# A linear-attention layer beside a long convolution on one core: dense scratch rows, D inside the filter, and a new table of priorities

## The chip, the cores and the metric

The kernel runs on one core of a Trainium2 chip. The time is device microseconds (us) of one execution; three executions of the kernel before are given, and one further execution was recorded by the hardware profiler. The engines are TensorE (PE; PEld is its loading of weights), VectorE (DVE), ScalarE (ACT), GpSimd (POOL) and SyncE (SP, which here issues all DMAs; SPq is its queue).

## The reference

Two independent parts, whose outputs stand side by side in the last axis (576 columns each, 2048 positions, bf16).

```python
# part A, 32 heads of 18, four segments of L = 512 positions
for s in range(4):
    logits = qs @ ks.T * scale + mask            # causal within the segment
    a_dot = softmax(logits) @ vs
    a_mem = (phi(qs) @ M) / (phi(qs) @ z + 1e-6) # phi(t) = t+1 if t>0 else exp(t)
    o = g * a_mem + (1 - g) * a_dot              # g = sigmoid(beta), one per head
    M += phi(ks).T @ vs ;  z += phi(ks).sum()
a = concat(o) @ wo
# part B, 576 channels, 2048 positions
kv = causal_conv4(k, shift_k) * v
y  = irfft(rfft(kv, 4096) * rfft(ssm_k, 4096))[:2048] + kv * ssm_D
b  = q * y
```

## The kernel before, in words

A small planner at build time holds both parts as one graph of operations. Each operation has its engines to choose from (a copy out of PSUM may go to VectorE or ScalarE), an estimated duration for each, and a priority: its place in its part's list, scaled to 0..0.9 for part A and 0..1 for part B. The planner picks, of the operations that could start soonest, the one with the lowest priority number, and so writes a fixed order for each engine. Nothing is reordered on the chip: an engine's instructions, and the DMAs on a queue, run in the order written.

Part A, for each segment s: x is loaded transposed (`xT`, L356, by transposing DMAs), q and k are projected (`pq`, L380), copied to SBUF (`q`, L245 on VectorE, L246 on ScalarE; these two lines are the copy helper for all tiles), stored to a DRAM scratch (`a_qk_scratch`, L368; k also to `a_k_scratch`, L372, from where it is read back transposed for the memory, `phiK`, L434) and read back so that each head lies on its own 32 partitions (`qk`, L408). V is projected on its own (`pv`, L417). The 32 heads are worked in four pairs of groups of four heads; the pair p holds the groups 2p and 2p+1. For each pair ten score tiles (`sc`, L483) go through an exponential (`PT`, L486, ScalarE, 160 in all) and masks on GpSimd (L491, 112 in all), then to the products with V (`po`, L530) and with the memory (`pn`, L537), whose sums ride along as a 19th column. `norm` gathers these sums from SBUF (`cs`, L555) and stores the outputs to `a_o_scratch` (L561, four DMAs per pair). `weights` inverts the sums on VectorE (L577), writes the factors to `a_r_scratch`, and a DRAM to DRAM copy (L588) spreads each factor over its head's 18 rows in `a_rx_scratch`. `dense` reads five tiles of 128 rows of outputs (`nt`, L604) and factors (`rt`, L606), multiplies (L612) and adds (L613), and `out_proj` multiplies with wo (`pout`, L624).

Part B splits 576 channels into three groups g of 192. The taps of the short convolution run on TensorE (`pc`, L816) over k that a transposing DMA has loaded (`kv`, L808). The long convolution is a Fourier transform in two stages: the first (`pf`, L839, two blocks of 256 columns per PSUM tile) gives `A_h` for the filter and `A_kv` for the signal. The second is done in 16 rows k1 per group, 48 in all:

```python
ph = self.f2(A_h, k1, 0, 1, Hs)                       # TensorE, L853
nc.vector.tensor_tensor(out=Hs[:, 1:3, :], in0=ph[:], in1=DI[:], op=ALU.add)     # L877: + D
eng.tensor_scalar(out=Hs[:, 0, :], in0=Hs[:, 2, :], scalar1=-1.0, ...)           # L881: -Im
px = self.f2(A, k1, 1, 0, X)                          # then a copy to X, L245 or L246
eng.tensor_tensor(out=Y.., in0=X.., in1=win, op=ALU.mult)       # L893, GpSimd, 4 x 192
eng.tensor_tensor(out=Y[:, 2:4, :], in0=Y[:, 0:2, :], in1=Y[:, 2:4, :], op=ALU.add)  # L898
```

L881 and L898 may go to GpSimd or VectorE; 45 of 48 stand on VectorE. The inverse of a row (`pi`, L865) writes over `A_kv`. When all 16 rows of a group are there, six blocks of transposes (`pt`, L913), a small product (`py`, L918) and the multiplication with q (`q_sb`, L921) end the group.

Buffers are rings: `big` (three) holds the index tables for the sines at the start, the `kv` tiles, `A_h` and `A_kv`, given out in the order in which the tiles are named; PSUM has two double slots for the scores and four single ones for all else.

## Time and profile before

| | |
|---|---|
| three executions | 377.89 us median, 376.07 to 379.33 |
| profiled execution | 379.78 us, of which 378.1 from the first to the last instruction |
| busy | PE 303.4, DVE 300.7, ACT 244.2, POOL 180.5 us |
| granted TensorE clock, mean | 0.905 |
| moved by DMA | 59.79 MB, 108604 packets, all from SyncE's queue |

Busy time is the union of an engine's instructions. A group's line gives the line of the program, the engine, what is written and read, the number, then busy us and mean ns of one, then the engine's idle time ahead of them with what ended it. A line of the timeline gives start and length in us. 1.7 us of the execution lie outside the span.

### The profile page before, as it was taken

Reading aid. Unit: us, or ns where it says so; the run is one execution under the profiler, and the core shown is the slowest. Engines: PE = TensorE matmul, PEld = TensorE weight load, DVE = VectorE, ACT = ScalarE, POOL = GpSimd, SP = SyncE. Lnnn points to the kernel's source line nnn. Section 1 sums busy time; section 2 is a strip of 40 time slices with the busy share of each in tenths; the row PEclk is TensorE's granted clock in tenths of the full one; section 3 lists DMA queues with packets and bytes.
Section 4 is the critical chain, followed back from the end, with each engine's and each line's share of the span. In section 5 each row is a group of like instructions: output and inputs, shape, how many; then the busy total and the mean of one; then the engine's idle time right before and its main releaser. Section 6 shows DMA issues by size and latency. Waiting matters only on the chain.

```text
span 378.1 us, 8137 instructions
## 1 busy us (share of the span) xinstructions
PE 303.4 (80%) x3030; PEld 171.8 (45%) x3052; DVE 300.7 (80%) x559; ACT 244.2 (65%) x337; POOL 180.5 (48%) x206
## 2 busy tenths in 40 slices
PE   0969695799988939799997988678997877789536
PEld 0524453355445514565453544234554443557413
DVE  8615574888999978877789997976889999998940
ACT  3621774688889846779876557685897886583202
POOL 7100120457678654415468535553638887673000
PEclk9978877899999997999998799898998998698957
DMA  6997889957325468639536877981543555224871
GB/s 138 224 213 196 186 170 176 234 154 194 98 71 112 83 183 188 177 104 226 150 103 153 185 214 211 236 252 53 124 129 101 166 146 150 80 81 135 248 217 63
DMA packets 108604, 59.79 MB, mean 158 GB/s; under 512 B 79508, under 2 KB 100692, under 8 KB 108564
## 3 DMA queue, kind: packets, MB, share of 16 engines
q1 hardware_dynamic: 108564, 59.26, 63.7%
q8 instruction: 24, 0.39, 0.4%
q14 instruction: 16, 0.13, 0.1%
HBM read 29.68 MB, written 23.82 MB: 142 GB/s over the span
## 4 chain that ended last, share of the span: by engine, by line
PE 33%; DVE 27%; DMA 16%; SPq 8%; ACT 7%; issue 7%; POOL 0%; DVEq 0%; ACTq 0%
DMA rt<-a_rx_scratch 6%; PE pout L624 5%; PE sc L483 5%; PE po L530 4%; PE pq L380 4%; DMA qk<-a_qk_scratch 4%; PE pp L853 3%; DVE Y L898 3%; ACT PT L486 3%; PE pi L865 3%; DVE nt L612 3%; DVE Hs L877 3%; SPq L808 2%; PE pf L839 2%; PE pv L417 2%
## 5 line engine op out<-in xcount | busy, mean ns | idle before, releaser
L486 ACT ACTIVATE PT<-sc 128x1024 bf16<-128x1024 f32 x160 | 157.7, 1034 | 39.1 <-PE sc L483 26.6
L491 POOL TENSOR_SCALAR_AFFINE_SELECT PT<-PT 128x512 bf16<-128x512 bf16 (+1 forms) x112 | 84.5, 768 | 101.7 <-ACT PT L486 95.9
L893 POOL TENSOR_TENSOR Y<-X,Hs 128x768 bf16<-128x768 bf16 x48 | 80.3, 1674 | 53.6 <-DVE X L245 19.8
L483 PE MATMUL sc<-qk 18*128 18x384 bf16 (+3 forms) x512 | 58.9, 316 | 9.7 <-ACT PT L486 4.8
L380 PE MATMUL pq<-xT,wqk 128*128 128x512 bf16 x161 | 47.0, 406 | 4.3 <-DVE ou L245 2.1
L483 PEld LDWEIGHTS <-qk 18*128 18x128 bf16 x512 | 16.2, 93 | 44.3 <-issue 38.8
L865 PE MATMUL pi<-Y,CST 128*128 128x192 bf16 x96 | 25.4, 265 | 10.5 <-DVE Y L898 8.7
L624 PE MATMUL pout<-wo_sb,od 128*128 128x288 bf16 x160 | 26.6, 319 | 8.6 <-DVE od L613 5.4
L839 PE MATMUL pf<-W1bd,xs 128*128 128x256 bf16 x144 | 27.3, 318 | 7.0 <-DVE V L245 3.1
L246 ACT CAST q<-pq 128x512 bf16<-128x512 f32 x23 | 13.5, 587 | 27.0 <-PE pq L380 20.9
L530 PE MATMUL po<-PT,V 128*32 128x256 bf16 (+3 forms) x512 | 27.1, 336 | 3.0 <-DVE Hs L877 1.8
L898 DVE TENSOR_TENSOR Y<-Y 128x384 bf16<-128x384 bf16 x45 | 28.6, 636 | 0.7 <-POOL Y L893 0.6
L877 DVE TENSOR_TENSOR Hs<-pp,DI 128x384 bf16<-128x384 f32 x48 | 26.3, 548 | 1.9 <-PE pp L853 1.7
L380 PEld LDWEIGHTS <-wqk 128*128 128x128 bf16 x180 | 17.3, 103 | 23.0 <-issue 9.8
L819 DVE TENSOR_TENSOR kv<-pc,kv 128x512 bf16<-128x512 f32 x20 | 13.5, 687 | 17.3 <-PE pc L816 17.3
L816 PE MATMUL pc<-kv,dg 128*128 128x512 bf16 x77 | 21.5, 422 | 5.8 <-ACT q L246 3.7
L853 PE MATMUL pp<-A_h,CS 128*128 128x192 bf16 x96 | 24.3, 256 | 1.8 <-DVE Hs L877 1.1
L853 PE MATMUL pp<-A_kv,CS 128*128 128x192 bf16 x96 | 24.5, 259 | 1.2 <-DVE X L245 0.4
L881 DVE TENSOR_SCALAR Hs<-Hs 128x192 bf16<-128x192 bf16 x45 | 23.5, 521 | 1.3
L246 ACT CAST oA<-pout 128x288 bf16<-128x288 f32 x25 | 10.0, 398 | 22.1 <-PE pout L624 21.2
L624 PEld LDWEIGHTS <-od 128*128 128x128 bf16 x160 | 16.5, 107 | 16.8 <-DVE od L613 6.6
L417 PE MATMUL pv<-wv,xT 128*128 128x288 bf16 x160 | 24.0, 293 | 0.0
(134 smaller groups left out, 575.4 us busy)
## 6 DMA issues: line engine op xcount, KB each, us to landing
qk<-a_qk_scratch SPq DMA_DIRECT2D x48, 108.0 KB
nt<-a_o_scratch SPq DMA_DIRECT2D x15, 256.0 KB
rt<-a_rx_scratch SPq DMA_DIRECT2D x15, 256.0 KB
a_o_scratch<-ou SPq DMA_DIRECT2D x48, 72.0 KB
xs<-in_B_ssm_k_dram SPq DMA_DIRECT2D x3, 768.0 KB
xs<-kv_scratch SPq DMA_DIRECT2D x3, 768.0 KB
q_sb<-in_B_q_dram SPq DMA_DIRECT2D x3, 768.0 KB
out_dram<-oA SPq DMA_DIRECT2D x16, 144.0 KB
```

The costliest lines, as they stand in the source:

```text
L380: nc.tensor.matmul(pq[:], lhsT=self.wqk[:, t, 128 * m:128 * m + P], rhs=xT[:, t, :], start=(t == 0), stop=(t == 4)) for t in range(5)],
L483: nc.tensor.matmul(ps[:, b, off:off + n], lhsT=qk[r, 2 + u, P * kt:P * kt + P], rhs=qk[r, u, P * kt:L], start=True, stop=True, tile_positi ...
L486: self.act(act_us(1024), lambda: nc.scalar.activation(out=dst(), in_=ps[:], func=ACT.Exp, scale=self.scale), r=[ps], w=[key])
L491: self.pool(0.2 + n * 0.13, lambda: nc.gpsimd.affine_select(out=ap(), in_=ap(), compare_op=ALU.is_ge, fill=0.0, base=0, pattern=[[0, n], [ ...
L530: nc.tensor.matmul(po[32 * j:32 * j + 32, P * kt:L], lhsT=V[:, kt, 19 * h:19 * h + 32], rhs=rhs, start=(kt == 0), stop=(kt == 3), tile_pos ...
L624: nc.tensor.matmul(ps[:], lhsT=o[:, t, P * qt:P * qt + P], rhs=self.wo[:, t, 288 * h:288 * h + 288], start=(t == 0), stop=(t == 4)) for t ...
L839: self.G.op([(PEQ, pe_us(256, 256), lambda cc=cc, ps=ps: [nc.tensor.matmul(ps[:, u, :], lhsT=xs[:, cc + u, :], rhs=self.W1[:].rearrange("p ...
L853: nc.tensor.matmul(pp[:, o, :], lhsT=tab[:, k1, :], rhs=A[:, 16 * n + k1, :], start=(n == 0), stop=(n == 1))
L865: nc.tensor.matmul(pp[:, o, :], lhsT=tab[:, k1, :], rhs=Y[:, 2 + n, :], start=(n == 0), stop=(n == 1))
L877: self.dve(dve_us(2 * GB), lambda: nc.vector.tensor_tensor(out=Hs[:, 1:3, :], in0=ph[:], in1=DI[:], op=ALU.add), r=[ph, (DI, 0), (DI, 1)], ...
L893: eng.tensor_tensor(out=Y[:].rearrange("p (x h) c -> p x h c", x=2), in0=X[:].unsqueeze(2).to_broadcast([P, 2, 2, GB]), in1=win, op=ALU.mult)
L898: return lambda: eng.tensor_tensor(out=Y[:, 2:4, :], in0=Y[:, 0:2, :], in1=Y[:, 2:4, :], op=ALU.add)
```

## The change: what it does

- Part B, row: D is added to the first tap of the filter (`xs`, L993, three small additions) ahead of its transform, so L877 and the tile `DI` go. The spectra of filter and signal are copied plain into one tile `HX` (two copies of 384, VectorE or ScalarE). No negative is made; instead of one sum of 384, GpSimd does a difference and a sum of 192 each (L953, L954), on GpSimd alone.
- Part B, first stage: four blocks per tile instead of two (36 copies of 1024 instead of 72 of 512), in the two double PSUM slots that the scores use.
- Part A: pair p holds the groups p and p+4. Scratches hold heads densely; k is read for `phiK` from the same scratch as q, and `a_k_scratch` goes. A pair's outputs, sums included, go to DRAM in one DMA; the sums are gathered from there (for the last pair from SBUF, as before). `dense` takes tiles of 7 heads (126 rows, the last 72) and reads the factors from `a_r_scratch`, each row 18 times; `a_rx_scratch` goes. wo is reordered to match by a copy through DRAM.
- Start: the first segment's x is one plain load, transposed on TensorE (20 transposes). Some loads may be issued from ScalarE's queue. The filter of group 0 is transformed ahead of the convolution taps.
- Planner: several estimated durations are raised or lowered, part A is scaled to 0..0.8, and two tables, keyed by stage, move priorities (`SHIFT`, 196 entries) and the choice of engine for copies (`BIAS`, 60 entries; the number is added to ScalarE's finishing time when the planner compares).

```diff
     def kloop(self, A_h, A, g, k1):
...
-        Hs = Tl(pl.H, [P, 3, GB], BF16, "Hs")
-        ph = self.f2(A_h, k1, 0, 1, Hs)
-        DI = self.DI
-        self.dve(dve_us(2 * GB), lambda: nc.vector.tensor_tensor(
-            out=Hs[:, 1:3, :], in0=ph[:], in1=DI[:], op=ALU.add), r=[ph, (DI, 0), (DI, 1)], w=[(Hs, 1)])
...
-        self.G.op([(POOLQ, 0.35, neg(nc.gpsimd)), (DVEQ, 0.17, neg(nc.vector))], r=[(Hs, 1)], w=[(Hs, 0)])
-
-        X = Tl(pl.X, [P, 2, GB], BF16, "X")
-        px = self.f2(A, k1, 1, 0, X)
-        self.copy(2 * GB, lambda: X[:], lambda: px[:], r=[px], w=[X, (A, "x", k1)])
+        HX = self.f2(A_h, A, k1)
...
-        self.G.op([(POOLQ, 1.75, mul(nc.gpsimd))], r=[X, (Hs, 0), (Hs, 1)], w=[Y])
-        self.G.op([(POOLQ, 0.95, add(nc.gpsimd)), (DVEQ, 0.33, add(nc.vector))], w=[Y])
+        def addsub():
+            nc.gpsimd.tensor_tensor(out=Y[:, 0, :], in0=Y[:, 0, :], in1=Y[:, 3, :], op=ALU.subtract)
+            nc.gpsimd.tensor_tensor(out=Y[:, 1, :], in0=Y[:, 1, :], in1=Y[:, 2, :], op=ALU.add)
+        self.pool(1.7, mul, r=[(HX, 0), (HX, 1)], w=[Y])
+        self.pool(1.1, addsub, w=[Y])
...
+    def f2(self, A_h, A, k1):
...
+            for x, src in enumerate((A_h, A)):
+                pp = self.psj([P, 1, L], "pp")
+                self.pe(pe_us(*[GB] * 4), lambda x=x, src=src, pp=pp: emit(0, src, pp), r=keys(src), w=[pp])
+                self.copy(2 * GB, lambda x=x: HX[:, x, :], lambda pp=pp: pp[:, 0, 0:2 * GB], r=[pp],
+                          w=[(HX, x)] + ([(A, "x", k1)] if x else []))
...
     def f1(self, xs, A):
+        w = 4 if F1D else 2
...
+            ps = Tl(self.pl.pss, [P, 4, 256], F32, "pf") if F1D else self.psj([P, 2, 256], "pf")
...
     def begin(self, g):
+        self.dve(0.15, lambda: nc.vector.tensor_tensor(out=xs[:, :, 0], in0=xs[:, :, 0], in1=self.Dt[:, n * g:n * g + n],
+                                                       op=ALU.add), r=["Dt"], w=[xs])
...
     def av(self, s, p, u):
-        hg = 2 * p + u
+        hg = p + 4 * u
...
     def norm(self, s, p):
+        dst = bass.AP(od.tensor, od[256 * p:256 * p + 1].offset, [[W, P], [128 * W, 2], [1, W]])
+        self.dma(256 * nk, lambda dq: dq.dma_start(out=dst, in_=ou[:].rearrange("p u k n -> p u (k n)")),
+                 r=[(ou, u, k) for u in range(2) for k in range(nk)], w=[("od", s, p)])
...
     def dense(self, s, t):
+        rsrc = bass.AP(rd.tensor, rd[7 * t:7 * t + 1].offset, [[W, nh], [0, DH], [1, W]])
...
+    def first_x(self, ident):
+        x = Tl(self.pl.big, [P, 4, D], BF16, "x0")
+        self.dma(576, lambda dq: dq.dma_start(out=x[:], in_=self.A_x[0, 0:L, :].rearrange("(t p) c -> p t c", p=P)), w=[x])
...
-    rank(G.ops[n0:n1], 0.0, 0.9)
-    rank(G.ops[n1:], 0.0, 1.0)
+    rank(G.ops[n0:n1], 0.0, 0.8, SHIFT)
+    rank(G.ops[n1:], 0.0, 1.0, SHIFT)
+    G.bias = BIAS
```

What the orders look like. SyncE's queue at the start, before (from its first row on):

```order
L294 DMA wqk<-in_A_wq_dram 128x4x576
L295 DMA wqk<-in_A_wq_dram 64x576
L356 DMA_TRANSPOSE xT<-in_A_x_dram 128x512 x5
L294 DMA wqk<-in_A_wk_dram 128x4x512
L295 DMA wqk<-in_A_wk_dram 64x512
...
L808 DMA_TRANSPOSE kv<-in_B_v_dram 128x2048
L808 DMA_TRANSPOSE kv<-in_B_k_dram 128x2048
L368 DMA a_qk_scratch_109<-q 128x512
```

And in the change (L373 is the plain load of x, L314 the reordering of wo, L402 the first q store):

```order
L297 DMA wqk<-in_A_wq_dram 128x4x576
L298 DMA wqk<-in_A_wq_dram 64x576
L314 DMA a_wo_scratch<-in_A_wo_dram 4x2x20736 x2
...
L297 DMA wv<-in_A_wv_dram 128x4x576
L298 DMA wv<-in_A_wv_dram 64x576
...
L373 DMA x_189<-in_A_x_dram 128x4x576
...
L860 DMA_TRANSPOSE kv<-in_B_k_dram 128x2048
L402 DMA a_qk_scratch_107<-q 128x512 x5
```

x has moved from third place to behind wv, with wk on another queue; four kv transposes instead of two stand ahead of the first store, and five stores follow at once.

GpSimd's last rows, before (Y is a row's product, PT a mask of the scores):

```order
L893 TENSOR_TENSOR Y<-X,Hs 128x768
L491 AFFINE_SELECT PT_5188<-PT_5188 128x4x128
L893 TENSOR_TENSOR Y<-X,Hs 128x768
L881 TENSOR_SCALAR Hs<-Hs 128x192
L491 AFFINE_SELECT PT_5230<-PT_5230 128x4x128 x2
L491 AFFINE_SELECT PT_5282<-PT_5282 128x4x128
L893 TENSOR_TENSOR Y<-X,Hs 128x768
L491 AFFINE_SELECT PT_5347<-PT_5347 128x4x128 x2
```

In the change the last mask stands here, and rows of part B still follow (seven products and eight pairs in all):

```order
L526 AFFINE_SELECT PT_5011<-PT_5011 128x4x128 x2
L953 TENSOR_TENSOR Y<-Y 128x192
L954 TENSOR_TENSOR Y<-Y 128x192
L947 TENSOR_TENSOR Y<-HX 128x768 x2
L953 TENSOR_TENSOR Y<-Y 128x192
L954 TENSOR_TENSOR Y<-Y 128x192
L947 TENSOR_TENSOR Y<-HX 128x768
```

The masks, which release part A's last products, have moved ahead of the last rows of part B.

VectorE in the middle of the program, where it works on rows of part B, before:

```order
L877 TENSOR_TENSOR Hs<-pp,DI 128x384
L881 TENSOR_SCALAR Hs<-Hs 128x192
L877 TENSOR_TENSOR Hs<-pp,DI 128x384
L881 TENSOR_SCALAR Hs<-Hs 128x192
L898 TENSOR_TENSOR Y<-Y 128x384
```

And in the change, where a row's VectorE work is its copies alone (L245 is the copy helper):

```order
L245 CAST HX<-pp 128x384
L978 TENSOR_TENSOR q_sb<-py,q_sb 128x64x8
L245 CAST HX<-pp 128x384 x2
L245 CAST q<-pq 128x512
L245 CAST ou<-pn 128x512
L245 CAST A_kv<-pi 128x2x192
```

The addition of D, the negation and the sum have left the engine.

More of the change, by code (lines that the diff above doesn't have):

```diff
@@ L557, in norm @@
[L557 to L565 removed]
+        W = nk * L
@@ new lines, in f2 @@
+        w = 4 if F1D else 2
+        keys = lambda a: [(a, cc) for cc in range(0, GB // 8, w)] + ["CS", "SN", "NSN", (HX, "claim")]
+        if HXD:
+            pp = Tl(self.pl.pss, [P, 2, L], F32, "pp")
+            self.pe(pe_us(*[GB] * 8), lambda: (emit(0, A_h, pp), emit(1, A, pp)), r=keys(A_h) + keys(A), w=[pp])
+            self.copy(4 * GB, lambda: HX[:], lambda: pp[:, :, 0:2 * GB], r=[pp], w=[(HX, 0), (HX, 1), (A, "x", k1)])
+        else:
+            for x, src in enumerate((A_h, A)):
[3 more added lines that the diff above has]
+                          w=[(HX, x)] + ([(A, "x", k1)] if x else []))
@@ L1009 @@
     n0 = len(G.ops)
-    a = PartA(tc, pl, G, A_x, A_wq, A_wk, A_wv, A_wo, A_beta, out)
+    a = PartA(tc, pl, G, b.ident, A_x, A_wq, A_wk, A_wv, A_wo, A_beta, out)
     a.build()
```

455 lines of the change are left out of this document (261 added, 194 removed), and 28 rows, old and new, of tables (BIAS, SHIFT).

## The prediction

> **What bounds the kernel now.** I read the head of the page first, for the span and the busy shares.
>
> ```profile
> span 378.1 us, 8137 instructions
> PE 303.4 (80%) x3030; PEld 171.8 (45%) x3052; DVE 300.7 (80%) x559; ACT 244.2 (65%) x337; POOL 180.5 (48%) x206
> ...
> PE 33%; DVE 27%; DMA 16%; SPq 8%; ACT 7%; issue 7%; POOL 0%; DVEq 0%; ACTq 0%
> DMA rt<-a_rx_scratch 6%; PE pout L624 5%; PE sc L483 5%; PE po L530 4%; PE pq L380 4%; DMA qk<-a_qk_scratch 4%; PE pp L853 3%; DVE Y L898 3%; ACT PT L486 3%; PE pi L865 3%; DVE nt L612 3%; DVE Hs L877 3%; SPq L808 2%; PE pf L839 2%; PE pv L417 2%
> ...
> L491 POOL TENSOR_SCALAR_AFFINE_SELECT PT<-PT 128x512 bf16<-128x512 bf16 (+1 forms) x112 | 84.5, 768 | 101.7 <-ACT PT L486 95.9
> ```
>
> The third line is the chain that ended last by engine, the fourth by line; the fifth is GpSimd's masks, with the idle time ahead of them and whom it was waiting for. Two engines are equally busy, TensorE and VectorE, and 24% of the chain is DMA and SyncE's queue. GpSimd has 198 us free and no place in the chain. An average over the span hides the stages, so I cut the span at the first and the last of the 160 exponentials of the scores (L486, the work that only ScalarE does). The timeline gives the two places; the second ends at 341.94 + 1.94 = 343.88.
>
> ```profile
> 43.80 3.79 ACT L486 ACTIVATE PT<-sc 128x1024 bf16<-128x1024 f32 x4
> 341.94 1.94 ACT L486 ACTIVATE PT<-sc 128x1024 bf16<-128x1024 f32 x2 [1.54 <-PE po L530]
> ```
>
> Busy time in these three stages (columns: stretch, its length, then PE, PEld, DVE, ACT, POOL busy with instruction counts, granted clock, DMA share, GB/s):
>
> ```profile
> 0.00:43.80 43.80, 29.11 (x155) 15.11 (x158) 22.98 (x62) 15.54 (x24) 8.57 (x24) 0.92 0.80 189
> 43.80:343.88 300.08, 254.71 (x2655) 142.41 (x2674) 259.57 (x466) 222.41 (x302) 170.73 (x180) 0.92 0.62 152
> 343.88:378.10 34.22, 19.57 (x222) 14.30 (x220) 18.12 (x34) 6.28 (x13) 1.25 (x2) 0.78 0.59 176
> ```
>
> The front (43.8 us) is held by loads: DMA share 0.80. The middle is 300 us, with VectorE at 86.5% and TensorE at 85%, GpSimd at 57%. The tail (34 us) is dense tiles and output. Inside the middle the limit moves:
>
> ```profile
> 80.00:140.00 60.00, 51.40 (x619) 28.65 (x622) 57.58 (x107) 48.61 (x63) 43.47 (x47) 1.00 0.50 123
> 140.00:200.00 60.00, 56.12 (x672) 31.97 (x677) 46.56 (x87) 46.11 (x63) 27.19 (x33) 0.94 0.66 156
> 200.00:260.00 60.00, 47.29 (x486) 24.56 (x487) 52.57 (x86) 36.55 (x52) 32.59 (x35) 0.89 0.75 196
> 260.00:340.00 80.00, 68.78 (x665) 40.60 (x664) 74.34 (x127) 63.49 (x86) 55.27 (x53) 0.91 0.44 120
> ```
>
> From 80 to 140 VectorE is 96% busy, from 260 to 340 93%: there it is the bound and TensorE stands at 86%. From 140 to 200, where VectorE has slack (78%), TensorE reaches 94%. That 94% is the mark for what TensorE does here when VectorE doesn't hold it.
>
> **The frequency rows of part B: what leaves VectorE.** One row (48 in all) is two spectra from TensorE (pp), a product on GpSimd (L893) and the inverse (pi). VectorE's instructions in it, and the two other groups whose number changes much:
>
> ```profile
> L898 DVE TENSOR_TENSOR Y<-Y 128x384 bf16<-128x384 bf16 x45 | 28.6, 636 | 0.7 <-POOL Y L893 0.6
> L877 DVE TENSOR_TENSOR Hs<-pp,DI 128x384 bf16<-128x384 f32 x48 | 26.3, 548 | 1.9 <-PE pp L853 1.7
> L881 DVE TENSOR_SCALAR Hs<-Hs 128x192 bf16<-128x192 bf16 x45 | 23.5, 521 | 1.3
> L245 DVE CAST X<-pp 128x384 bf16<-128x384 f32 x35 | 19.1, 547 | 2.4 <-PE pp L853 2.4
> L245 DVE CAST A_h<-pf 128x512 bf16<-128x512 f32 x23 | 15.3, 683 | 1.7 <-PE pf L839 1.5
> L245 DVE CAST A_kv<-pf 128x512 bf16<-128x512 f32 x19 | 12.6, 684 | 0.8 <-PE pf L839 0.7
> L245 DVE CAST q<-pq 128x512 bf16<-128x512 f32 x13 | 8.9, 685 | 4.8 <-PE pq L380 4.8
> L245 DVE CAST oA<-pout 128x288 bf16<-128x288 f32 x7 | 3.1, 453 | 0.1
> ```
>
> The addition of D, the negation and the sum of products go, and so do these copies: 28.6 + 26.3 + 23.5 + 19.1 + 15.3 + 12.6 = 125.4 us. In their place VectorE gets 75 plain copies HX of 384 elements (75 x 0.547 = 41.0) and 18 copies of first-stage results of 1024 elements. No row has that copy; from below, one of 512 elements is 0.68, from above, two of them are 1.37; the line through 384 (0.547) and 512 (0.684) gives 1.23, which I take: 22.1 us. By the written order VectorE further takes 14 more q copies (9.6) and 21 more oA copies (9.5), which leave ScalarE. The sum is 125.4 - 82.2 = **43 us less on VectorE**: 216 of the middle's 260 if all of it is taken there. The multiplication by D moves into the first tap of the filter (three additions of 24 columns each, where a copy of 288 columns takes 0.45 us) and is put at nothing. ScalarE loses the 35 copies named and gains 8 HX copies and 5 early DMA issues; at 222 us in the middle it was not the bound and gets no worse.
>
> **What GpSimd gets.** The sum of products becomes two instructions of 192 elements each, always on GpSimd: 96 of them. The bounds come from these rows (ns: min/median/max):
>
> ```profile
> L898 DVE TENSOR_TENSOR Y<-Y x45: 341/357/1794, 74.0 to 343.8; 128x384 bf16<-128x384 bf16 x45
> L898 POOL TENSOR_TENSOR Y<-Y x3: 907/912/1003, 206.2 to 286.5; 128x384 bf16<-128x384 bf16 x3
> L881 POOL TENSOR_SCALAR Hs<-Hs x3: 740/753/797, 132.8 to 337.6; 128x192 bf16<-128x192 bf16 x3
> L893 POOL TENSOR_TENSOR Y<-X,Hs x48: 1627/1638/2100, 71.2 to 340.7; 128x768 bf16<-128x768 bf16 x48
> ```
>
> Half of the 384-element addition is 0.46, the one instruction of 192 elements is 0.75, and the line through 384 (0.912) and 768 (1.638) gives 0.55. I take 0.57, near the additions of the same kind: 96 x 0.57 = 55 us, and GpSimd stands at about 228 us. 8 of the 48 pairs come after the last mask, so the middle has 171 + 40 x 1.14 - 11 (7 products that move to the tail) = 205 us of 271: 76%, not the bound as long as the work is spread.
>
> A rule speaks against this edit. The Trainium skill, page "GPSIMD Engine Reference", section "4.1 Engine selection", sends two-input elementwise work to VectorE and calls GpSimd about twice as slow. The rows agree and are harsher: 912 against 357 ns, a factor of 2.6. By the rule alone the edit would cost 55 us of engine time to save 28.6, which is the third rival below; the busy shares, which the rule doesn't weigh, say that GpSimd has the room.
>
> **What TensorE keeps.** The matmuls are the same but for 20 transposes of x in the front (xT comes by TensorE instead of a transposing DMA). The order moves some out of the middle: 48 pp, 36 pi and 24 pf fewer, 16 pc more between the first and the last score. Busy time of all of L853 (pp), L865 (pi), L839 (pf) and L816 (pc), in this order:
>
> ```profile
> 0.00:378.10 378.10, 46.41 (x384) 32.62 (x384) 0.91 0.64 158
> 0.00:378.10 378.10, 26.24 (x192) 16.04 (x192) 0.91 0.64 158
> 0.00:378.10 378.10, 27.34 (x144) 13.65 (x144) 0.91 0.64 158
> 0.00:378.10 378.10, 21.52 (x77) 8.15 (x80) 0.91 0.64 158
> ```
>
> 48 x 0.121 + 36 x 0.137 + 24 x 0.190 - 16 x 0.279 = 5.8 + 4.9 + 4.6 - 4.5 = 10.8, so the middle's TensorE work falls from 254.7 to 244 us. With VectorE at 216, ScalarE near 210 and GpSimd at 205, TensorE is then alone at the top. I put it at 90%, between the 85% of now and the 94% of the stretch where VectorE has slack: **middle 244 / 0.90 = 271 us**, 29 less. The bounds are 94% (260) and 82% (298), where the wait for VectorE is only replaced by one for slots: the first-stage tiles now share the two PSUM slots of the scores.
>
> **DMA edits.** Heads are stored dense, k is stored once, a pair's output goes out in one DMA instead of four, and the factors are spread to 18 rows each by the load itself: the copy a_rx_scratch goes, and SyncE issues fewer DMAs. In the chain rt stands at 6% (23 us) and the queue at 8% (30 us). But before the factors the sums are now fetched from DRAM behind the store, so only in the last segment is a hop saved. In the middle I put all this at nothing, since TensorE's 244 us remain whatever DMA does; what it may bring there is part of rival 1, what it may hide is in rival 2.
>
> **Front.** These rows carry it (SPq is SyncE's DMA queue):
>
> ```profile
> 0.79 0.46 SPq L294 DMA_DIRECT2D wqk<-in_A_wq_dram  x1
> 1.95 6.47 SPq L356 DMA_TRANSPOSE xT<-in_A_x_dram  x5
> 10.04 2.34 PE L380 MATMUL pq<-xT,wqk 128*128 128x512 bf16 x5
> 14.33 5.16 SPq L808 DMA_TRANSPOSE kv<-in_B_v_dram  x1
> 19.54 2.56 SPq L808 DMA_TRANSPOSE kv<-in_B_k_dram  x1
> 22.20 0.53 SPq L368 DMA_DIRECT2D a_qk_scratch<-q  x1
> 0.00:20.00 20.00, 10.67 (x61) 5.86 (x63) 15.12 (x41) 9.62 (x11) 8.57 (x24) 1.00 0.81 180
> ```
>
> Now x is there for the first projection at 10 us. In the change x is one plain load, but it waits for a buffer of the ring that the sine tables use, and it stands on SyncE behind wq, the copy of wo, wv and small ones, while wk and the filter load go out on ScalarE's queue. By the tiles' sizes that is 3.4 MB ahead of 0.6; at the 180 GB/s of the first 20 us x lands at 22, and at best, if it passes the rest, at about 12. Then come 20 transposes and some 27 us of TensorE work (29.1 now, with 24 pf instead of 16 pc): first score between 41 and 51. In return all four kv transposes still stand ahead of the first q store, but stores are one DMA instead of two or three. I take **44 us**, as now, with 39 to 51 as bounds.
>
> **Tail.** GpSimd's last 7 products and 8 pairs stand behind the last mask: 7 x 1.64 + 16 x 0.57 = 20.6 us, where now nothing does. Behind them one inverse and six blocks of transposes (pt, py), then output:
>
> ```profile
> 346.17 1.25 PE L913 MATMUL pt<-ident,A_kv 128*128 128x128 bf16 x16
> 359.70 0.61 PE L918 MATMUL py<-Psibd,Ct 128*128 128x64 bf16 x8 [1.72 <-DVE Ct L245]
> 374.40 0.40 ACT L246 CAST oA<-pout 128x288 bf16<-128x288 f32 x1 [0.17 <-PE pout L624]
> ```
>
> The blocks took 346.2 to 360.3 now, 14 us; the end came 3.3 us after the last copy (378.1 - 374.8). In the change attention's dense path runs beside GpSimd, one DRAM hop shorter, so it isn't added: 1.3 for masks + 20.6 + 14 + 3.3 = **39 us**, against 34.2 now. Bounds: 34 if the blocks run closer together, 44 with 0.75 for each addition.
>
> **Sum.** 44 + 271 + 39 = 354 us of span. The profiled execution was 379.78 us, 1.7 outside the span; it lies 1.9 above the median of 377.89. So 354 + 1.7 - 1.9 = **354 us**, 6% faster. The bounds of the three terms alone give 333 (39 + 260 + 34) to 393 (51 + 298 + 44), but these don't fall together. A difference under 1% can hardly be told from none here (the runs shown range from 376.07 to 379.33).
>
> **Rivals.** (1) TensorE reaches 94% in the middle and x lands early: 40 + 260 + 36 = 336. For it: VectorE's waiting for GpSimd goes too (medians of 357 against means of 636 on L898). Against: 200 to 260, where DMA is at 0.75 and neither engine is full.
> (2) No gain: TensorE's idle 15% wasn't VectorE's doing, and the new order brings new waits: 82%, so 44 + 298 + 36 = 378. For it: from 200 to 260 TensorE is at 79% with VectorE at 88%. Against: 80 to 140.
> (3) Slower, by GpSimd's queue. A row's two additions stand in order ahead of masks; masks release the products po, and these the score buffers. 40 pairs of 1.14 us are 46 us; if all of it is on the path, 44 + 271 + 46 + 40 = 401. From half of it on (23 us) nothing is left of the gain. For it: each row now passes GpSimd twice before the inverse. Against: GpSimd sat idle for 101.7 us ahead of masks, 95.9 of it for exponentials (L491 above), so it has slack there.
>
> **How the numbers follow.** Forecast (343 to 366) 0.58, rival 1 0.17, rival 2 0.12, rival 3 0.13. The range takes in the forecast, rival 2 and most of rival 1: 335 to 379. Faster by over 1%: forecast, rival 1 and a small part of rival 2, 0.76; within 1%: 0.12; slower: 0.12.
>
> **What would show it.** VectorE near 258 us and GpSimd near 228 with additions at 0.5 to 0.75; the last exponential at about 315; TensorE the only engine at 90% between; a first projection later than 15 us; GpSimd busy for 20 us after the last mask. The forecast is wrong if the last exponential comes after 335, if masks wait behind the additions, or if x lands after 25.

## The result and the profile after

The changed kernel takes **363.7 us** (median of four, 362.1 to 366.1) beside 378.6 us of the kernel before: a ratio of 0.962, 95% interval 0.953 to 0.970. The profiled execution took 362.62 us, with a span of 360.9 at a mean granted clock of 0.923. Executions over 1.5% longer than the fastest of the same kernel are left out of the medians and ratios below, and the profile of the run with x first is of such an execution (granted clock 0.878, where the others of that kernel had 0.906 to 0.919), so only its start is read.

The head of the page of the changed kernel, and its chain that ended last, by engine:

```profile
PE 296.2 (82%) x3048; PEld 171.8 (48%) x3072; DVE 274.0 (76%) x486; ACT 233.9 (65%) x296; POOL 227.2 (63%) x294
...
PE 47%; DMA 17%; DVE 17%; issue 5%; SPq 3%; POOL 3%; ACTq 3%; ACT 3%; DVEq 0%; POOLq 0%
```

VectorE's share of the chain has fallen from 27% to 17%, TensorE's has risen from 33% to 47%. Cut again at the first and the last exponential (columns as before: stretch, length, busy PE, PEld, DVE, ACT, POOL, granted clock, DMA share, GB/s):

```profile
0.00:50.01 50.01, 27.54 (x185) 17.60 (x187) 32.93 (x90) 14.83 (x18) 7.80 (x23) 1.00 0.76 176
50.01:318.60 268.59, 243.38 (x2605) 134.84 (x2627) 210.69 (x350) 210.68 (x264) 196.40 (x245) 0.93 0.61 159
318.60:360.90 42.30, 25.28 (x262) 19.32 (x259) 30.40 (x47) 8.42 (x16) 22.99 (x27) 0.78 0.38 120
```

The middle lost 31.5 us (300.1 to 268.6). The front took 6.2 back (43.8 to 50.0), the tail 8.1 (34.2 to 42.3). The groups that answer to those of before, VectorE's copies and GpSimd's new sums:

```profile
L245 DVE CAST HX<-pp 128x384 bf16<-128x384 f32 x75 | 38.9, 548 | 7.0 <-PE pp L910 6.3
L245 DVE CAST q<-pq 128x512 bf16<-128x512 f32 x27 | 18.5, 687 | 13.7 <-PE pq L411 12.7 <-PE sc L518 0.9
...
L526 POOL TENSOR_SCALAR_AFFINE_SELECT PT<-PT 128x512 bf16<-128x512 bf16 (+1 forms) x112 | 80.8, 738 | 68.3 <-ACT PT L521 67.1 <-PE pi L934 1.1
L954 POOL TENSOR_TENSOR Y<-Y 128x192 bf16<-128x192 bf16 x48 | 29.6, 617 | 0.0
L953 POOL TENSOR_TENSOR Y<-Y 128x192 bf16<-128x192 bf16 x48 | 28.4, 592 | 1.4
```

The sums cost 0.59 and 0.62 us each on GpSimd. When it stands idle ahead of a mask, it still waits for an exponential (67.1 of 68.3 us). A mask that stands behind a sum would not show as idle time; but of the waits listed in the change, none of TensorE's or ScalarE's is for a mask. What TensorE does wait for is the sums: 10.9 us ahead of the inverses (pi).

**Where the front's 6 us went.** The timeline of the start (ACTq and SPq are the queues on which ScalarE and SyncE issue DMAs; a line gives start and length):

```profile
2.82 7.52 ACTq L297 DMA_DIRECT2D wqk<-in_A_wk_dram  x1
10.95 1.28 ACT L762 ACT_TABLE_LOAD   x1 [10.95 <-issue]
...
8.37 0.43 SPq L297 DMA_DIRECT2D wv<-in_A_wv_dram  x1
16.16 0.52 SPq L298 DMA_DIRECT2D wv<-in_A_wv_dram  x1
17.61 0.67 SPq L846 DMA_DIRECT2D Dt<-in_B_ssm_D_dram  x1
18.39 0.52 SPq L373 DMA_DIRECT2D x<-in_A_x_dram  x1
...
23.59 1.89 PE L895 MATMUL pf<-W1bd,xs 128*128 128x256 bf16 x8 [7.19 <-DVE xs L993]
28.61 1.28 PE L383 MATMUL pt<-ident,x 128*128 128x128 bf16 x20
30.60 0.38 PE L411 MATMUL pq<-xT,wqk 128*128 128x512 bf16 x1
```

ScalarE stands for 7.5 us in the issue of one small load of wk and starts its first table at 10.95 (0.78 before). SyncE stands between the two pieces of wv from 8.8 to 16.2. Dt and x, ordered behind them, go out at 17.6 and 18.4 (Dt also waits for GpSimd to clear its tile, at 17.1); the filter's first stage waits for Dt, the transposes of x stand behind it, and the first projection comes at 30.6, where it was at 10.0.

**The tail**: GpSimd's last mask and last sum, the last inverse copied and the last output, from the timeline:

```profile
319.25 1.27 POOL L526 TENSOR_SCALAR_AFFINE_SELECT PT<-PT 128x512 bf16<-128x512 bf16 x2
341.07 0.99 POOL L954 TENSOR_TENSOR Y<-Y 128x192 bf16<-128x192 bf16 x1
342.79 0.48 ACT L246 CAST A_kv<-pi 128x384 bf16<-128x384 f32 x1 [6.93 <-PE pi L934]
356.70 0.40 ACT L246 CAST oA<-pout 128x288 bf16<-128x288 f32 x1 [0.22 <-PE pout L667]
```

Two steps of the chain that ended last, in order of time:

```profile
330.37 7.49 DMA a_r_scratch<-cs
337.94 5.49 DMA rt<-a_r_scratch
```

GpSimd works 21.5 us behind the last mask (320.5 to 342.1). Beside it runs attention's way through DRAM: factors stored from 330.4, read back by 343.4. The last inverse is copied by 343.3, and the last TensorE work of both, the blocks and pout, shares the 14 us from 343 to 357. From 330.4 on the chain that ended last goes through the two DMAs, not through GpSimd.

### The profile page after: what moved, and what is told of

It is laid out like the page before. It is cut to its first block, busy times and chain, and to the rows that moved or that the text cites. A ratio compares the mean times of both kernels' runs of the same rounds, so it can differ in the third digit from the quotient of the medians.

```text
span 360.9 us, 7982 instructions
## 1 busy us (share of the span) xinstructions
PE 296.2 (82%) x3048; PEld 171.8 (48%) x3072; DVE 274.0 (76%) x486; ACT 233.9 (65%) x296; POOL 227.2 (63%) x294
## 4 chain that ended last, share of the span: by engine, by line
PE 47%; DMA 17%; DVE 17%; issue 5%; SPq 3%; POOL 3%; ACTq 3%; ACT 3%; DVEq 0%; POOLq 0%
PE sc L518 9%; DMA rt<-a_r_scratch 7%; PE pq L411 6%; PE pout L667 5%; PE pp L910 5%; PE po L568 5%; DMA a_r_scratch<-cs 4%; PE pc L869 4%; PE pf L895 3%; PE pv L450 3%; PE pi L934 3%; ACTq L297 2%; DVE HX L245 2%; POOL Y L947 2%; DMA Dt<-in_B_ssm_D_dram 2%
## 5 line engine op out<-in xcount | busy, mean ns | idle before, releaser
L521 ACT ACTIVATE PT<-sc 128x1024 bf16<-128x1024 f32 x160 | 157.9, 1029 | 33.0 <-PE sc L518 21.5
L526 POOL TENSOR_SCALAR_AFFINE_SELECT PT<-PT 128x512 bf16<-128x512 bf16 (+1 forms) x112 | 80.8, 738 | 68.3 <-ACT PT L521 67.1
L947 POOL TENSOR_TENSOR Y<-HX 128x768 bf16<-128x768 bf16 x48 | 81.9, 1712 | 14.2 <-PE pi L934 9.4
L518 PE MATMUL sc<-qk 18*128 18x512 bf16 (+3 forms) x512 | 60.6, 316 | 5.8 <-ACT PT L521 5.2
L245 DVE CAST HX<-pp 128x384 bf16<-128x384 f32 x75 | 38.9, 548 | 7.0 <-PE pp L910 6.3
L954 POOL TENSOR_TENSOR Y<-Y 128x192 bf16<-128x192 bf16 x48 | 29.6, 617 | 0.0
L953 POOL TENSOR_TENSOR Y<-Y 128x192 bf16<-128x192 bf16 x48 | 28.4, 592 | 1.4
L245 DVE CAST q<-pq 128x512 bf16<-128x512 f32 x27 | 18.5, 687 | 13.7 <-PE pq L411 12.7
L667 PE MATMUL pout<-wo_sb,od 126*128 126x288 bf16 (+1 forms) x160 | 23.6, 291 | 0.2 <-issue 0.2
L910 PEld LDWEIGHTS <-CS 128*128 128x128 bf16 x192 | 18.9, 101 | 9.8 <-issue 9.0
L655 DVE TENSOR_TENSOR nt<-nt,rt 126x1024 bf16<-126x1024 bf16 (+1 forms) x15 | 13.6, 904 | 10.3 <-DMA rt<-a_r_scratch 10.3
L245 DVE CAST A_kv<-pi 128x384 bf16<-128x384 f32 x33 | 17.9, 550 | 3.8 <-PE pi L934 3.3
L450 PEld LDWEIGHTS <-xT 128*128 128x128 bf16 x160 | 16.3, 106 | 9.1 <-issue 2.9
```

The lines of the kernel that those rows point to most:

```text
L245: return self.G.op([(DVEQ, dve_us(n, 0.53 if bf else 1.042), lambda: nc.vector.tensor_copy(out=out(), in_=in_())), (ACTQ, act_us(n), lambd ...
L450: nc.tensor.matmul(pv[:], lhsT=xT[:, t, P * tt:P * tt + P], rhs=self.wv[:, t, 288 * h:288 * h + 288], start=(t == 0), stop=(t == 4)) for t ...
L518: nc.tensor.matmul(ps[:, b, off:off + n], lhsT=qk[r, 2 + u, P * kt:P * kt + P], rhs=qk[r, u, P * kt:L], start=True, stop=True, tile_positi ...
L521: self.act(act_us(1024), lambda: nc.scalar.activation(out=dst(), in_=ps[:], func=ACT.Exp, scale=self.scale), r=[ps], w=[key])
L526: self.pool(0.2 + n * 0.13, lambda: nc.gpsimd.affine_select(out=ap(), in_=ap(), compare_op=ALU.is_ge, fill=0.0, base=0, pattern=[[0, n], [ ...
L667: nc.tensor.matmul(ps[:], lhsT=o[0:K, t, P * qt:P * qt + P], rhs=self.wo[0:K, t, 288 * h:288 * h + 288], start=(t == 0), stop=(t == 4)) fo ...
```

## The experiments

The theory on record: the gain is VectorE's time in the rows. The rivals: the order that the two tables write, or part A's DMA edits.

### The parts: rows, tables, the rest

The rows alone, in the kernel before (no table, old first stage, old part A); the planner writes a new order for them:

```diff
-        self.dve(dve_us(2 * GB), lambda: nc.vector.tensor_tensor(out=Hs[:, 1:3, :], in0=ph[:], in1=DI[:], op=ALU.add), ...)
+        self.copy(2 * GB, lambda: HX[:, 0, :]..., lambda: ph[:], r=[ph], w=[(HX, 0)])
...
-        self.G.op([(POOLQ, 0.95, add(nc.gpsimd)), (DVEQ, 0.33, add(nc.vector))], w=[Y])
+        self.G.op([(POOLQ, 1.1, addsub)], w=[Y])
```

> The kernel before with the new row form alone: D in the first filter tap, two plain copies into HX, difference and sum of 192 on GpSimd; loads, part A, first stage and planner as before. Theory (VectorE was the bound in the middle, and the rows free it): VectorE loses L877, L881 and L898 (78.4 us) and takes at most 48 more copies of 0.547 (26.3), so about 50 us less; GpSimd gains about 55. The middle keeps its 254.7 us of TensorE, at 90% that is 283 instead of 300: 358 to 366 us in all. Rival 1 (the gain is the order that the two tables write): 372 or more. Rival 2 (the gain is part A's DMA edits): 372 or more.

Measured: 371.8 us, ratio 0.980 (0.973 to 0.988). Less than the theory asked (358 to 366), just under the rivals' bound. The page's busy line:

```profile
PE 304.9 (83%) x3052; PEld 173.1 (47%) x3052; DVE 264.8 (72%) x471; ACT 246.2 (67%) x338; POOL 224.9 (61%) x294
```

And its middle, in the same columns as above:

```profile
33.77:335.62 301.85, 263.85 (x2757) 149.31 (x2757) 231.03 (x397) 223.31 (x305) 208.15 (x260) 0.90 0.63 157
```

VectorE does fall by 36 us (300.7 to 264.8, where the theory said about 50), to 77% of the middle. But TensorE reaches 87%, not 90, and at a lower granted clock (0.90 instead of 0.92). The middle isn't shorter than before (301.9 against 300.1 us), though it holds 102 more matmuls: the first exponential comes at 33.8 instead of 43.8, with work moved behind it. The rows, in the order that the planner then writes, were worth 7 us.

The other three corners: old rows and old first stage in the changed kernel, with the tables cut to the entries of the start, and with the whole tables; and new rows with the tables cut. A row of the tables that names a stage not in the program has no effect. The two with old rows also have one tile in the buffer ring `cs`, where the change has two, and one in `DI`, where the kernel before has two. The edit of the tables:

```diff
+    keep = {k: v for k, v in SHIFT.items() if first(k)}
...
-    rank(G.ops[n0:n1], 0.0, 0.8, SHIFT)
-    rank(G.ops[n1:], 0.0, 1.0, SHIFT)
-    G.bias = BIAS
+    rank(G.ops[n0:n1], 0.0, 0.8, keep)
+    rank(G.ops[n1:], 0.0, 1.0, keep)
+    G.bias = {None: 0.4, 'tr0': 0}
```

> The changed kernel with the old row form and the old first stage (D added to the spectrum on VectorE, negation, sum of 384, two blocks per PSUM tile), and with the tables cut to the entries of the start; part A's edits and the loads of the start stay. Theory: VectorE is back at 295 to 305 us and the middle at 295 or more, with the longer front of the change: 375 to 390 us. Rival 2 (part A's DMA edits carry the gain): 368 or less.

> The changed kernel with SHIFT and BIAS cut to the entries that concern the start (loads, first projections); everything else as changed. Theory: the rows' share of the gain stays, the tables add a smaller part: middle 270 to 285 us, 364 to 374 in all. Rival 1 (the tables carry the gain): middle 295 or more, 378 or more.

> The changed kernel with the old row form and the old first stage as in the earlier run without rows, but with both tables kept whole (entries whose stage has another name now have no effect). Theory (rows and tables need each other: with VectorE at 310 or more no order fills TensorE): 380 to 395 us, the tables bring less than half of the 28 us that they bring with the new rows. Rival 1 (the order alone carries the gain): 371 us or less, that is 364 and the 7 us that the rows were worth in the kernel before.

| | old rows | new rows |
|---|---|---|
| order and part A of before | 378.6 (before) | 371.8 |
| part A of the change, tables cut | 398.5, ratio 1.050 (1.041 to 1.059) | 390.2, ratio 1.030 (1.017 to 1.044) |
| part A of the change, tables whole | 405.8 (two executions: 403.6 and 407.9) | 363.7 (the change) |

The lines with part A of the change also have its start, its estimated durations and its scaled priorities; there "old rows" means the old first stage too. Each expectation misses in part. With old rows and tables cut the time lies above the theory's 375 to 390 us and VectorE at 321.6 us above its 295 to 305; rival 2's 368 us are far off. With new rows and tables cut the middle is in the theory's range (283.6 of 270 to 285), the time in rival 1's (378 or more). With old rows and whole tables the time lies above both (380 to 395; 371 or less).

Rival 2 falls as the only cause: with part A's edits and the old rows the kernel is slower than before in either order (398.5 and 405.8 against 378.6). What part A's edits do by themselves isn't shown, since the start and the planner's numbers changed with them, and no run has the new rows and the tables without them. The theory alone misses too: the rows bring 7 and 8 us in the first and second line of the table and 42 in the third. And rival 1 alone misses: the tables bring 27 us with the new rows and cost 7 with the old ones. Rows and tables work together. What the tables do is seen in the stages of the run with the new rows and the tables cut:

```profile
48.41:332.04 283.63, 252.50 (x2590) 136.66 (x2590) 220.94 (x376) 196.65 (x231) 180.53 (x234) 0.89 0.59 151
332.04:388.40 56.36, 34.32 (x300) 26.55 (x297) 41.81 (x65) 4.45 (x9) 35.06 (x38) 0.73 0.28 87
```

The middle is 15 us longer than with the whole tables, and 14 us more stand in the tail, where 35 us of GpSimd's rows are left over after the last exponential.

### VectorE's time with the order kept

First the sums of the rows on VectorE, with the planner free to reorder (it then counts them there, at 0.5 us a pair); then the same with every other instruction kept in its place. The edit of both:

```diff
-            nc.gpsimd.tensor_tensor(out=Y[:, 0, :], in0=Y[:, 0, :], in1=Y[:, 3, :], op=ALU.subtract)
-            nc.gpsimd.tensor_tensor(out=Y[:, 1, :], in0=Y[:, 1, :], in1=Y[:, 2, :], op=ALU.add)
+            nc.vector.tensor_tensor(out=Y[:, 0, :], in0=Y[:, 0, :], in1=Y[:, 3, :], op=ALU.subtract)
+            nc.vector.tensor_tensor(out=Y[:, 1, :], in0=Y[:, 1, :], in1=Y[:, 2, :], op=ALU.add)
```

> The changed kernel with a row's difference and sum (96 instructions of 192 elements) on VectorE instead of GpSimd; the planner rewrites the order with it. Theory: VectorE gains 96 x 0.25 to 0.33 (half of 357 ns undisturbed, half of the mean 636 stretched) = 24 to 32 us and stands at about 300, GpSimd loses 55; VectorE is the bound of the middle again: 370 to 380 us. Rival (elementwise work belongs on VectorE, and GpSimd's 55 us and its 21 us behind the last mask are on the path): 360 us or less.

> The changed kernel with the 96 instructions L953 and L954 issued on VectorE at the same places of the program, nothing replanned, order of all other instructions kept. Theory (VectorE's time is what counts in the middle): VectorE 24 to 32 us up, to about 300, and 372 to 385 us in all. Rival (in the earlier test with the sums on VectorE it was the rewritten order that cost the time): 361 to 367 us. Rival (GpSimd's additions are on the path): below 360.

Measured: 385.2 us (ratio 1.013, 1.007 to 1.020) and 381.7 us (1.012, 1.003 to 1.021). The theory's range held with the order kept (372 to 385), and the reordered kernel lay 5 us above its own (370 to 380); the rivals fall. VectorE went from 274.0 to 299.7 us, and with the order kept the time rose by 18: the whole gain is gone. The middle of the run with the order kept, and stretches of 2 us around one stall:

```profile
48.80:336.43 287.63, 260.50 (x2627) 141.12 (x2627) 232.97 (x428) 211.93 (x264) 151.25 (x166) 0.87 0.58 149
...
120.00:122.00 2.00, 1.94 (x21) 1.13 (x17) 1.97 (x5) 2.00 (x4) 1.29 (x1) 1.00 0.42 138
122.00:124.00 2.00, 0.00 (x0) 0.00 (x0) 2.00 (x3) 1.44 (x3) 1.81 (x3) 1.00 0.18 59
124.00:126.00 2.00, 0.57 (x4) 0.41 (x5) 2.00 (x3) 0.00 (x0) 1.52 (x1) 0.87 0.07 16
126.00:128.00 2.00, 2.00 (x12) 1.32 (x9) 1.82 (x4) 0.00 (x0) 0.00 (x0) 0.50 0.00 0
128.00:130.00 2.00, 2.00 (x14) 1.00 (x12) 1.95 (x6) 1.04 (x2) 0.00 (x0) 0.78 0.00 0
```

And VectorE's and TensorE's timeline there:

```profile
122.89 1.14 DVE L953 TENSOR_TENSOR Y<-Y 128x192 bf16<-128x192 bf16 x1
123.95 1.68 DVE L954 TENSOR_TENSOR Y<-Y 128x192 bf16<-128x192 bf16 x1
...
121.17 0.78 PE L450 MATMUL pv<-wv,xT 128*128 128x288 bf16 x5
124.08 0.26 PE L934 MATMUL pi<-Y,CST 128*128 128x192 bf16 x1 [2.14 <-DVE Y L953]
125.68 0.32 PE L934 MATMUL pi<-Y,NSNT 128*128 128x192 bf16 x1 [1.34 <-DVE Y L954]
126.97 1.41 PE L450 MATMUL pv<-wv,xT 128*128 128x288 bf16 x5
```

Two additions, which took 0.24 us each at 120.2 and 120.4, before GpSimd's next product (120.7), take 1.14 and 1.68 while GpSimd is at work. TensorE waits 2.1 and 1.3 us for them, and from 126 its granted clock is 0.50: five matmuls of pv take 1.41 instead of 0.78 us. This stall costs twice, once as waiting and once as a slow stretch behind it. The Trainium skill, page "TensorE: Matmul & The Clock Gate", section "HAM oscillation — how this bites in real kernels", describes this: a wait of some 3.4 us returns the clock to half, and the next work starts slowly. The trace agrees here: of the 4.0 us from 122 to 126 TensorE is busy 0.57, and 0.50 follows. But that doesn't account for all slow time: from 292 to 312 the clock is 0.50 with TensorE busy 20.00 of 20.00 us, and what holds it low there isn't shown. Nor is it shown how much of the 18 us is the clock's: the profiled execution had a mean clock of 0.872 and a span of 380.0 us, two others of the same kernel 0.910 and 0.897 with 379.0 and 383.8.

So TensorE's busy share says less than it seems to. Busy time times granted clock, the work at full clock, is the same in the middle of both kernels: 243.4 x 0.93 = 226 in the change, 260.5 x 0.87 = 227 here. Both show TensorE at 90.6% (243.4 of 268.6, 260.5 of 287.6), but in work at full clock per time it is 84% and 79%. The kernel before had 254.7 x 0.92 = 234 of 300.1, 78%, and the run with the rows alone 263.9 x 0.90 = 237 of 301.9, 79%.

### The front

From here on the planner's choice is kept as it is, and single operations are moved in its list `plan` before the instructions are written; everything else keeps its place on every engine. First the small load of wk:

```diff
+    plan.remove(wkt)
+    plan.insert(wv + 1, (wkt[0], SPQ, [], a.wkt_op.alts[0][2]))
```

> The changed kernel with its order kept on every engine; only the small load of wk's first 64 columns (128x4x64 and 64x64) moves from ScalarE's queue to SyncE's, behind wv. Theory for the longer front (ScalarE stands in the issue of this load until 10.9 us, the sine of W1bd and with it fpat's buffer, Dt and x come late): the first table load moves from 10.95 to about 3.5, x is issued at 10 to 13 instead of 18.4, the first exponential comes at 42 to 46 instead of 50.0, and the end follows: 356 to 360 us. Rival (the front is held by the bytes ahead of x on the queues): the first exponential stays within 2 us, 362 to 366 us.

Measured: 366.1 us, ratio 0.967 (0.961 to 0.972), first exponential at 51.3. The theory that ScalarE's stall sets the front falls; the rival's first exponential (within 2 us of 50.0) holds, its 362 to 366 us nearly, but not by the bytes that it named: from 13 to 20 us the DMA engines move 51 GB/s. Its rows show why:

```profile
2.82 1.28 ACT L769 ACT_TABLE_LOAD   x1 [2.82 <-issue]
...
10.19 0.58 SPq L301 DMA_DIRECT2D wqk<-in_A_wk_dram  x1
17.80 0.49 SPq L302 DMA_DIRECT2D wqk<-in_A_wk_dram  x1
19.83 0.52 SPq L379 DMA_DIRECT2D x<-in_A_x_dram  x1
```

ScalarE is free at 2.8, 8 us earlier. Now SyncE stands behind its piece of wk until 17.8, and x goes out later than before. Next, x, wq and Dt first on SyncE, x in a buffer that nothing else uses at that time, in addition to this:

```diff
+    a.x0.make = lambda: setattr(a.x0, "tile", pl.sb.tile(a.x0.shape, a.x0.dtype, tag="od0", name="x0"))
+    first = [by[a.x_op], by[a.wq_op], by[b.dt0_op], by[b.dt1_op]]
+    plan = first + [e for e in plan if e not in first + tr]
+    i = [e[0] for e in plan].index(b.CS_op) + 1
+    plan = plan[:i] + tr + plan[i:]
```

> The edit of the run before, and x loaded first on SyncE into a buffer that nothing else uses, Dt's memset and load directly behind wq, the 20 transposes of x and their three copies behind the sine of CS; the order of everything else kept. Theory: x lands by 9 us, the first projection comes at 20 to 24 instead of 30.6 (now behind the transposes of CS and the filter's first stage), the first exponential at 36 to 42: 350 to 357 us. Rival (loads and head transfers through DRAM set the first scores, not x): the first exponential not before 46, 360 us or more.

Measured: 364.9 us, ratio 0.967 (0.960 to 0.975), first exponential at 49.1: the theory misses, the rival's numbers hold. x is transposed from 6.4 us on, but nothing follows from it:

```profile
9.21 0.37 SPq L301 DMA_DIRECT2D wv<-in_A_wv_dram  x1
20.91 0.54 SPq L302 DMA_DIRECT2D wv<-in_A_wv_dram  x1
...
20.92 0.27 DVE L1005 TENSOR_TENSOR xs<-xs,Dt 128x24 bf16<-128x24 bf16 x1 [6.72 <-DMA xs<-in_B_ssm_k_dram]
25.62 0.23 ACT L332 ACTIVATE omg<-beta 128x32 f32<-128x32 bf16 x1 [9.49 <-DMA beta<-in_A_beta_dram]
```

The filter, issued at 2 us, lands at 20.9; SyncE is held in wv until then, and ScalarE stands 9.5 us before the load of beta, with the copies of the first stage behind it in its order. Then wo's two DMA steps late, alone, and everything together, with the load of beta moved up behind Dt as well:

```diff
+    late = [by[a.wod_op], by[a.wo_op]]
+    plan = [e for e in plan if e not in late]
+    for e, lab in zip(late, (("ld", 0, 0), ("x", 1))):
+        i = max(i for i, f in enumerate(plan) if f[0].label == lab) + 1
+        plan.insert(i, e)
```

> The changed kernel with the two DMA steps of wo (the copy into its reordered scratch, 8 pieces of 41472 bytes, and the load from there) moved on SyncE's queue behind the first heads' loads and behind the next segment's x; the order of everything else kept. Theory (those large pieces sit on a few of the DMA engines, and every load issued behind them ends only when those few have caught up: between 13 and 20 us the DMA share is 0.2): the hole closes, Dt and x land 6 to 9 us earlier, the first exponential comes at 41 to 45 instead of 50.0: 355 to 360 us. Rival (the loads' bytes set the front): first exponential within 2 us of 50, 362 to 366 us.

> The edits of the two runs on the front and of the run before together (wo late; x, wq, Dt and beta first on SyncE; the small wk load on SyncE; x transposed behind the sine of CS), order of the rest kept. Theory: the filter lands by 14 us, the first projection comes at 19 to 23, the first exponential at 37 to 42, and the whole gain shows at the end: 350 to 357 us. Rival (a shorter front is given back in the middle, since TensorE there has the same work at the same rate and the tail is set elsewhere): first exponential as said, but 360 us or more.

Alone: 368.2 us, ratio 0.971 (0.965 to 0.977), first exponential at 48.1: the theory's 41 to 45 falls, and the rival's 2 us just hold, but not its 362 to 366 us. Together: **360.0 us**, ratio 0.952 (0.945 to 0.958), first exponential at 39.1. The stretch from 13 to 20 us (DMA share is the last column but one), first in the change:

```profile
13.00:20.00 7.00, 1.89 (x16) 1.62 (x16) 4.51 (x13) 5.14 (x5) 4.40 (x12) 1.00 0.21 46
```

With x first:

```profile
13.00:20.00 7.00, 1.30 (x13) 1.03 (x10) 1.10 (x7) 3.11 (x3) 0.16 (x2) 1.00 0.28 95
```

With wo late alone:

```profile
13.00:20.00 7.00, 1.89 (x16) 1.62 (x16) 3.37 (x13) 4.00 (x5) 3.33 (x11) 1.00 0.18 18
```

With everything:

```profile
13.00:20.00 7.00, 5.66 (x53) 4.46 (x51) 6.35 (x16) 5.60 (x7) 0.16 (x2) 1.00 0.83 191
```

The DMA engines stand mostly idle in the first three, at 18 to 95 GB/s, so bytes don't set this stretch; when all holds are gone they move 191. The holds stand in a row, and taking one away shows the next: ScalarE's issue, SyncE's issue behind wo's large pieces, Dt behind GpSimd's work on W1bd, beta. With wo late alone it is the third that holds SyncE: it issues nothing from 8.0 to 16.2 us, until GpSimd has cleared Dt's tile (15.9), and the share is 0.18. The 0.21 and 0.28 while wo stands early would be four of sixteen DMA engines still at work. The Trainium skill, page "DMA: Bandwidth & Descriptors", section "Rules for kernel authors", says that an outermost dimension of a size under 16 confines a DMA to that many engines; each half of wo's copy has 4 there. No run changes that shape alone, and the run with x first differs from the last one by beta's place too, so this reading is argued, not shown; the 0.18 without wo shows that a share as low comes about in another way too.

Of the 11 us that the first exponential gained, 3.7 came out at the end. The middle of that run took the rest back:

```profile
39.08:316.11 277.03, 246.53 (x2605) 135.25 (x2627) 212.94 (x350) 211.37 (x264) 195.30 (x245) 0.92 0.61 157
```

TensorE has the same work there (246.5 x 0.92 = 227), spread over 277.0 instead of 268.6 us. Theory and rival share the verdict: the time lies at 360, the rival's bound. Most of the loss lies in one place. The 11th exponential starts at 49.7 us, 11.4 earlier than in the change, the 16th at 77.4, only 4.3 earlier. Between them ScalarE's copy of q waits for a store to DRAM to land, while the DMA engines are busy throughout (a share of 1.14):

```profile
60.00:70.00 10.00, 7.38 (x64) 4.58 (x64) 8.68 (x14) 5.95 (x9) 2.25 (x3) 1.00 1.14 267
...
71.33 0.58 ACT L250 CAST q<-pq 128x512 bf16<-128x512 f32 x1 [4.81 <-DMA a_qk_scratch<-e]
```

In the change this wait is 2.33 us. The run with wo late alone loses 5.6 us at the same place, with a wait of 4.78; of the runs with wo early, that on the small load of wk gains 0.4 there and that on the last sums (below) loses 1.9. So the loss goes with the late loads of wo (49.5 us here), which add to what the DMA engines move then. No run has the early start with wo early, so this is read from the traces, not tested. One step more, the first four projections ahead of the filter's first stage:

```diff
+    qk = [by[b.SN_op]] + [e for e in plan if e[0].label in (("qk", 0, 0), ("qk", 0, 5), ("qk", 0, 2), ("qk", 0, 7), ("ld", 0, 0))]
+    plan = [e for e in plan if e not in qk]
+    i = min(i for i, e in enumerate(plan) if e[0].label == "tab" and e[1] == PEQ)
+    plan = plan[:i] + qk + plan[i:]
```

> The run before, and the first four projections (pq, their copies, stores and the first heads' loads) ahead of the transposes of CS and of the filter's first stage on every engine, the kv transposes behind them on SyncE. Theory (TensorE then starts at 14 to 16 us instead of waiting for the filter): first exponential at 35 to 41, 348 to 356 us. Rival (the order of TensorE behind it, with pv and pc ahead of the first score, sets the first exponential): within 1.5 us of the run before.

Measured: 363.2 us, ratio 0.958 (0.952 to 0.964), first exponential at 45.0. Both expectations miss. TensorE starts its projections at 12.4, but the kv transposes now stand behind the q stores on SyncE and start at 23.5 instead of 14.7, and pc, which stands ahead of the first scores, comes later. The version with all edits of the front but this one is the best of all that ran. Its interval overlaps that of the change (0.945 to 0.958 against 0.953 to 0.970): it is likely ahead by a per cent, not surely.

### The tail

```diff
+            e = nc.vector if g == 2 and k1 >= 8 else nc.gpsimd
-            nc.gpsimd.tensor_tensor(out=Y[:, 0, :], in0=Y[:, 0, :], in1=Y[:, 3, :], op=ALU.subtract)
+            e.tensor_tensor(out=Y[:, 0, :], in0=Y[:, 0, :], in1=Y[:, 3, :], op=ALU.subtract)
...
```

> The changed kernel with the difference and sum of the last eight rows alone (16 of the 96 instructions, those behind the last mask) on VectorE, order of everything else kept. Theory (the tail is the length of GpSimd's rows and the six blocks behind them): GpSimd needs 12 instead of 21 us behind the last mask, the last copy of the inverse comes at 333 to 336 instead of 343.3, the tail is 36 to 40 instead of 42.3: 358 to 362 us. Rival (the tail is attention's way through DRAM: factors stored at 330, read at 343, last output at 357): the inverse ends as early, the end comes within 1.5 us, 362 to 366 us.

Measured: 365.2 us, ratio 0.963 (0.958 to 0.968); tail 42.65 instead of 42.30. The end says that the rival is right, but its inverse was to end early and didn't (346.1 us). VectorE and ScalarE near the end of this run:

```profile
343.85 0.69 DVE L655 TENSOR_TENSOR nt<-nt,rt 126x1024 bf16<-126x1024 bf16 x1 [0.65 <-DMA rt<-a_r_scratch]
344.46 0.26 DVE L954 TENSOR_TENSOR Y<-Y 128x192 bf16<-128x192 bf16 x1
345.63 0.48 ACT L246 CAST A_kv<-pi 128x384 bf16<-128x384 f32 x1 [6.22 <-PE pi L934]
```

The last sums now stand in VectorE's order behind a dense product that waits for the factors from DRAM, so the rows inherit attention's wait. The way of the factors is as long as GpSimd's 21.5 us; what the tail would be with the rows out of the way isn't shown.

## Why the prediction was right, and where not

- **Middle: 271 said, 268.6 measured.** TensorE's 244 us are 243.4, its 90% are 90.6; VectorE 216 there is 210.7, GpSimd 205 is 196.4 (73%). The terms hold. The reason holds by half, so that the number came out is in part luck. That VectorE's time counts is shown (25.7 us more of it cost 18 us with the order kept). That freeing it brings TensorE to 90% by itself is not: the rows alone gave 87% at a lower clock, a middle no shorter than before, and 7 us. The step "TensorE is then alone at the top, I put it at 90%" silently took an order that uses the freed time; with the tables cut the same rows gave 283.6 in the middle and 390.2 us in all. The prediction had put the order at 10.8 us of work moved out of the middle; the tables are worth 27. Its mark of 94% also counted slow time: in the two stretches of 60 us that it compares, 56.12 x 0.94 is 88% and 51.40 x 1.00 is 86%, so in work at full clock VectorE's slack was worth 2 points, not 8.
- **Front: 44 said (39 to 51), 50.0 measured.** The mis-sized term. "A first projection later than 15 us" was right and too mild: 30.6. The sum let x land between 12 and 22 by bytes over GB/s, and put five DMA issues on ScalarE at nothing. One of them took 7.5 us; x was issued at 18.4 behind two other waits, and its transposes stood behind the filter's first stage, which waited for Dt. When x landed isn't seen; TensorE did not wait for it at 28.6.
- **Tail: 39 said (34 to 44), 42.3 measured.** GpSimd behind the last mask: 20.6 said, 21.5 measured. Mis-sized is what comes then: attention's dense path "runs beside GpSimd, so it isn't added", but its output shares TensorE and VectorE with the blocks from 343 to 357.
- **VectorE in all: 258 said, 274.0 measured.** The listed groups fell as said. But smaller groups grew, by some 11 us: the durations of all VectorE instructions add to 328.9 us before and 296.7 in the change, 32 less and not 43. And the sum subtracted durations, while busy time is their union: 28.2 us of them overlapped before, 22.6 in the change.
- **GpSimd: 228 said, 227.2 measured**; sums at 0.59 and 0.62 instead of 0.57.
- **DMA edits at nothing in the middle**: no run has them alone. They are part of the two runs with old rows, which differ in other things too.
- **Rivals.** Rival 3 (sums ahead of masks) isn't seen: neither TensorE nor ScalarE is listed as waiting for a mask. The sums cost 10.9 us ahead of the inverses, where VectorE's sum of before cost 8.7. Rival 2's price, 82% of TensorE, shows in no run as a busy share; in work at full clock the middles stand lower, at 78% before and 84% in the change.

Front and tail erred by +6 and +3, the middle by -2: the sum erred by 7 of the span's 361, and by 10 in the median of the time, since the profiled execution lay 1.1 below the median here and not 1.9 above it as before. The last exponential ended at 318.6 where 315 was said.

## What to carry to other kernels

Time freed on an engine is worth what the written order makes of it: the same rows were worth 7 us in one order and 42 in another, and a table of priorities that fits one program cost 7 us in its neighbour. Judge a stretch that TensorE fills by busy time times granted clock per length, since the busy share stayed at 90.6% while the stretch grew by 19 us. At a start with many loads, move the holds together: taken singly or in part, the edits moved the first exponential by 2 us at most, and together by 11, of which the end kept a third.

## What was not expected of the hardware

- A DMA issue can hold an engine for long: 7.52 us for one load of 128x4x64 on ScalarE, and 7.4 to 11.3 us between two issues on SyncE, on the same queue that at 0.8 us took 0.5 us for an issue.
- An addition of two SBUF tiles of 192 columns took 0.24 us on VectorE alone and up to 1.7 us beside GpSimd's work, and TensorE, which had waited for it, then ran at half its clock for about 3.4 us (from the clocks 0.87, 0.50 and 0.78 of three stretches of 2 us).
- TensorE's clock can stay at half while it is shown busy: 20.00 of 20.00 us at 0.50. Its work at full clock came out as 226 or 227 us in the middle of three kernels with the same order, whose middles were 268.6, 277.0 and 287.6 us long and whose busy times differed by 17 us.
